# Token-major attention turned by DMA for three of eight batches, in a fused linear-attention and bilinear-FFN kernel

## Chip, cores, metric

One core of one Trainium2 chip. The metric is the device time of one execution in microseconds (us), median over several. All runs that are compared are fast unless a slow one is named (slow: over 1.5% above the fastest run of the same kernel). A *turn* below is a DMA transpose; an *eviction* takes a result out of a bank of PSUM; a DMA has *landed* when its semaphore says so; *head* and *tail* are the first microseconds of an execution and the part after the last matmul starts.

## The reference

```python
# q, k, v: (8 batches, 8 heads, 576 tokens, 64), fp32
kv  = einsum('bhsd,bhse->bhde', k, v)
out = einsum('bhsd,bhde->bhse', q, kv)
rms = sqrt(mean(out * out, axis=-1, keepdims=True) + 1e-06)
x   = (out / rms * g_norm) as (4608 tokens, 512)      # heads side by side
y   = ((x @ w_a) * (x @ w_b)) @ w_out                 # 512 -> 1536 -> 512
```

## The kernel before

The FFN is done in blocks of 512 tokens; blocks 1 to 8 use a seven-product scheme for 2 x 2 block matrices, with differences of x and of the weights made on VectorE. The attention of later batches is woven in between. TensorE (PE) needs x with the 512 features on the partitions, in ring buffers `xp`. So the attention is computed feature-major, two heads (128 features) and 288 tokens at a time:

```python
def x_mm(self, p, h, ps):            # out, transposed: features x 288 tokens
    nc.tensor.matmul(ps[:, 0:HF], lhsT=self.kvd[:, p, :], rhs=self.q[p][:, h*HF:(h+1)*HF], ...)
def sq_op(self, p, h, sq):           # ScalarE
    nc.scalar.activation(sq, self.x_ps[p, h][:, 0:HF], AF.Square)
def s_mm(self, p, h, ps):            # mean over 64 features: a product with a matrix of 1/64
    nc.tensor.matmul(ps[:, 0:HF], lhsT=ones, rhs=self.sq[p, h], start=True, stop=True)
def rs_op(self, p, h, rs):           # ScalarE
    nc.scalar.activation(rs, self.s_ps[p, h][:, 0:HF], AF.Abs_reciprocal_sqrt, bias=eps_t)
def xt_op(self, p, h):               # VectorE: x * g * rs, straight into xp
    nc.vector.scalar_tensor_tensor(out=xcols(...), in0=self.x_ps[p, h][:, 0:HF],
        scalar=g_col, in1=self.rs[p, h], op0=ALU.mult, op1=ALU.mult)
```

That is 8 times two matmuls of 288 columns for each batch. q comes through DRAM: cast by GpSimd's DMA, then turned by one DMA transpose on SyncE's queue (SP). The order on each engine is fixed ahead of time by a small list scheduler, `Plan`, which simulates the engines with durations given in the program; at run time only semaphores wait. PSUM is dealt out so:

```python
PB, PA, PO = Pool(banks[0:4]), Pool(banks[5:8]), Pool(banks[4:5])   # blocks, attention, output
...
issue_us, q_us, ld["kv_us"] = (15.4, 4.3, 13.0) if dep is None else (9.0, 5.0 if b == 3 else 1.8, 13.0)
ld["n"] = plan.add("POOL", issue_us, prio, issue, [(dep["qn"], 8.0)] if dep else [], [ld["k"], ld["v"]])
```

`kv_us` is the time after the load's issue at which the scheduler thinks k and v have landed.

Of the kernel before, what the change touches and what calls it, by code (L numbers as in the profile page):

```python
# [8 lines left out]
FP32 = mybir.dt.float32  # L9
# [6 lines left out]


class Pool:
    def __init__(self, tiles):
        self.tiles, self.holder = tiles, [None] * len(tiles)  # L20

    def pick(self, gone=()):
        best = (INF, 0)
        for i, b in enumerate(self.holder):
            if i not in gone:
                best = min(best, (b.freed() if b else 0.0, i))
        return best


# [11 lines left out]
class Buf:  # L41
# [6 lines left out]
    def take(self, t=0.0):  # L48
        r = self.ring
        i = r.pool.pick()[1]  # L50

        self.got = max(r.when(), r.pool.pick()[0])
        self.tile = r.pool.tiles[i]
        r.pool.holder[i] = self
        r.held = [b for b in r.held if b.freed() > t] + [self]
        return self

# [78 lines left out]
def kernel(  # L136
# [11 lines left out]
    nc = tc.nc  # L148
# [33 lines left out]
    EH = d_model // 2  # L182

    const = ctx.enter_context(tc.tile_pool(name="const", bufs=1))
    scr_pool = ctx.enter_context(tc.tile_pool(name="scr", bufs=B, space=bass.MemoryType.DRAM))
    psum = ctx.enter_context(tc.tile_pool(name="psum", bufs=1, space=bass.MemoryType.PSUM))
    ctx.enter_context(tc.manual_schedule())

    def sb(name, shape, dt):
        return const.tile(shape, dt, name=name)  # L190
# [15 lines left out]
    as_t = sb("as", [128, 4, NJ, 256], FP16)  # L206
    b_ts = [sb(f"c{i}", [128, 4, 2, NMAX], FP16) for i in range(2)]
    u_t = sb("u", [128, 6, 2, NMAX], FP32)
    sq_ts = [sb(f"sq{i}", [128, HF], BF16) for i in range(3)]
    rs_ts = [sb(f"rs{i}", [128, HF], FP32) for i in range(3)]  # L210
    o_ts = [sb(f"o_sb{i}", [128, 4, d_model], FP32) for i in range(2)]

# [203 lines left out]
        ]  # L416

    T0 = 20.0
    plan = Plan({"PE": 5.7, "DVE": 3.3, "ACT": 2.7, "SP": 5.0, "POOL": 22.5, "V": 0.0})
    PB, PA, PO = Pool(banks[0:4]), Pool(banks[5:8]), Pool(banks[4:5])  # L420
    RX, RY, RO = Ring(PB, 2), Ring(PB, 2), Ring(PO)
    RQ, RS = Ring(PA, 2), Ring(PA, 2)
    RU, RB, RAB = Ring([u_t[:, i] for i in range(6)]), Ring(b_ts), Ring(ab_ts)
    RT, RAS = Ring([T_t[:, i] for i in range(5)]), Ring([as_t[:, i] for i in range(4)])
    RSQ, RRS, ROS = Ring(sq_ts), Ring(rs_ts), Ring(o_ts)
    RK, RV, RQT, RKD = Ring(k_ts), Ring(v_ts), Ring(qT_ts), Ring(kvd)
    normed = {}
# [14 lines left out]
    def slices(at, win, extra):  # L442
        w0, w1 = win
        for i in range(2 * NP):
            p, h = divmod(i, 2)
            pr = w0 + (w1 - w0) * i / (2 * NP)
            x, s = ((Buf(RX), Buf(RY)) if at.b == 0 and i % 3 == 1 else (Buf(RQ), Buf(RS)))
            sq, rs = Buf(RSQ), Buf(RRS)
            ta = at.b * S + h * HF
            war = [  # L450
                n
                for j, (a, b) in enumerate(blocks_of)
                if a < ta - R + HF and b > ta - R
                for n in readers.get(j, ())
            ]
            n1 = plan.add(
                "PE", mm_us(1, HF), pr,
                lambda p=p, h=h, x=x: at.x_mm(p, h, x.tile), extra(p), [x], at.qt,
            )
            n2 = plan.add(  # L460
                "ACT", act_us(HF), pr, lambda p=p, h=h, b=sq: at.sq_op(p, h, b.tile), [n1], [sq]
            )
            n3 = plan.add(
                "PE", mm_us(1, HF), pr,
                lambda p=p, h=h, s=s: at.s_mm(p, h, s.tile), [n2], [s], [sq],
            )
            s_done[at.b] = n3
            n4 = plan.add(
                "ACT", act_us(HF, True), pr,
                lambda p=p, h=h, b=rs: at.rs_op(p, h, b.tile), [n3], [rs], [s],  # L470
            )
            normed[at.b, p, h] = plan.add(
                "DVE", dve_us(HF) + 0.06, pr,
                lambda p=p, h=h: at.xt_op(p, h), [n4] + war + ([g_n] if at.b == 0 else []), (), [x, rs],
            )

    def early_batch(b, win):
# [35 lines left out]
            done[p] = [n2, n4]  # L513
        slices(at, win, lambda p: done[p])

    def late_batch(b, load, win):
        at = Attn(b)
        w0, w1 = win
        kb, vb, qb = load["k"], load["v"], load["q"]
        kd = Buf(RKD)  # L520
        at.qt = [qb, kd]

        def view(t):
            return t[:, 0 : H * (NCH + 1) * D].rearrange("p (h c d) -> p h c d", h=H, d=D)

        s = Buf(RS)

        def kv_mm():
            kv_ps = s.tile[:].rearrange("p (a e) -> p a e", a=NP)
            for c in range(NCH + 1):  # L530
                for p in range(NP):
                    hs = slice(2 * p, 2 * p + 2)
                    nc.tensor.matmul(  # L533
                        kv_ps[:, p, :],
                        lhsT=kb.tile[:, c, hs, :],
                        rhs=view(vb.tile)[:, hs, c, :],
                        start=(c == 0 and p == 0),
                        stop=(c == NCH and p == NP - 1),
                    )

        n = plan.add(
            "PE", 1.15, w0, kv_mm, [(load["n"], load["kv_us"]), plan.at(w0 - 3)], [s, kd], [kb, vb]
        )

        def kv_out():
            kv_ps = s.tile[:].rearrange("p (a e) -> p a e", a=NP)
            at.kvd = kd.tile
            nc.scalar.copy(at.kvd[0:D, :, 0:D], kv_ps[0:D, :, 0:D])
            nc.scalar.copy(at.kvd[D:, :, D:], kv_ps[D:, :, D:])
            for p in range(NP):  # L550
                at.q[p] = qb.tile[:, p, :]

        m = plan.add("ACT", 0.75, w0, kv_out, [n], (), [s])
        slices(at, (w0 + 0.12 * (w1 - w0), w1), lambda p: [m, (load["qn"], 8.0)])


    def load_node(b, prio, dep):
        ld = {"k": Buf(RK), "v": Buf(RV), "q": Buf(RQT)}
        scr = scr_pool.tile([NP, S, 2, D], BF16, name="scr", tag="scr")

        def issue():
            if dep is not None:
                nc.gpsimd.tensor_copy(gate_t, dep["q"].tile[0:1, 0, 0:1])
            qv = q[b].rearrange("(p hl) s d -> hl s p d", hl=2)
            for hl in range(2):
                nc.gpsimd.dma_start(  # L566
                    out=scr[:, :, hl, :].rearrange("p s d -> s p d"), in_=qv[hl]
                )
            kt = ld["k"].tile
            ks = k[b, :, 0:SA, :].rearrange("h (sp c) d -> sp h c d", c=NCH)  # L570
            for c in range(NCH):
                nc.gpsimd.dma_start(out=kt[:, c], in_=ks[:, :, c, :])  # L572
            nc.gpsimd.dma_start(out=kt[0:SB, NCH], in_=k[b, :, SA:S, :].rearrange("h sp d -> sp h d"))
            for n, src in (("v", v),):
                t = ld[n].tile[:, 0 : H * (NCH + 1) * D].rearrange(
                    "p (h c d) -> p h c d", h=H, d=D
                )
                nc.gpsimd.dma_start(
                    out=t[:, :, 0:NCH, :],
                    in_=src[b, :, 0:SA, :].rearrange("h (sp c) d -> sp h c d", c=NCH),  # L580
                )
                nc.gpsimd.dma_start(
                    out=t[0:SB, :, NCH, :], in_=src[b, :, SA:S, :].rearrange("h sp d -> sp h d")
                )

        def transpose():
# [2 lines left out]
                in_=scr[:].rearrange("a s h d -> (a s) (h d)"),  # L589
            )  # L590

        issue_us, q_us, ld["kv_us"] = (15.4, 4.3, 13.0) if dep is None else (9.0, 5.0 if b == 3 else 1.8, 13.0)

        ld["n"] = plan.add(
            "POOL", issue_us, prio, issue, [(dep["qn"], 8.0)] if dep else [], [ld["k"], ld["v"]]
        )
        ld["qn"] = plan.add(
            "SP", 2.5, prio, transpose, [(ld["n"], q_us)], [ld["q"]]
# [95 lines left out]
    def wino_block(bi, win, wsum):  # L694
# [26 lines left out]
        for j in range(NJ):  # L721
# [4 lines left out]
            tkb = plan.add("V", 0.0, pr - 3, lambda: None, (), [bb])  # L726
            X = Buf(RQ if (bi == nb and j % 3 == 2) or (bi == 1 and j % 3 == 1) else RX)
            Y, Z = Buf(RY), Buf(RO if bi == 1 and j % 2 else RY)
            u1, u2, u3 = Buf(RU), Buf(RU), Buf(RU)
            wts = [(wa_t, sums["a"]), (wb_t, sums["b"])]  # L730

# [291 lines left out]
    for b in range(2, B):  # L1023
        t = b * S / N0
        at_win[b] = (max(53.0, st[int(t) - 1] + (t % 1) * L[int(t) - 1] - 18), st[int(t)] - 22 + (t % 1) * 12)
    loads = {2: load_node(2, 22.5, None)}
    wo_n = load_wo(loads[2])
    for b in range(3, B):
        loads[b] = load_node(b, at_win[b - 1][0], loads[b - 1])
    gb = Buf(RQ)  # L1030
    g_in = plan.add(
        "PE", 0.07, 8.5, lambda: nc.tensor.transpose(gb.tile[:, 0:1], g_row, one), [plan.at(6.4)], [gb]
# [10 lines left out]
    for bi in range(1, nb + 1):  # L1043
        o_win = (st[bi] + 1.0, st[bi + 1] - 1.0) if bi < nb else (st[bi] + O_A, st[bi + 1] + O_B)
        if bi == 1:
            o_std(ab, muls, (o_win[0] + 4.0, o_win[1] + 4.0))
            osum = out_sums(st[2] - 10)
        else:
            o_block(bi - 1, ab, muls, osum, o_win, 2, (RO, RY, RY), 1)
        for b in needs[bi]:  # L1050
            late_batch(b, loads[b], at_win[b])
        ab, muls = wino_block(bi, (st[bi], st[bi + 1]), wsum)
    o_block(
        nb, ab, muls, osum, (st[nb + 1], st[nb + 1] + o_us[nb]), NJ // 2,
# [38 lines left out]
```

## Time and profile before

| | before |
|---|---|
| median of the timed runs | 299.75 us (298.81 to 300.07, 4 runs) |
| span of the profiled run | 297.8 us |
| busy: PE, VectorE (DVE), ScalarE (ACT) | 98%, 79%, 65% |
| gaps between matmul starts, 40 to 130 us / 130 to 258 us | 1.50 / 0.25 us |
| from the start of the last matmul to the end | 4.96 us |

The gaps, here and below, are worked out from the trace: the distance from the start of one matmul to the start of the next, less its columns / 2.4 GHz, less 2.5 ns, summed where it is positive. They tell more than "busy", which models the ends of matmuls and fills such gaps. PE is fed almost without a break, so the count of columns sets the time.

### The profile page before, as it was taken

The numbers are of one execution on the slowest core, as the hardware profiler recorded it, in microseconds if no ns is written. First come the engines' busy times: TensorE is split into PE (matmuls) and PEld (weight loads), VectorE is DVE, ScalarE is ACT, GpSimd is POOL, SyncE is SP. The second block draws the span as 40 slices with busy tenths as digits, with TensorE's granted clock in tenths as the row PEclk, the third lists the DMA queues.
The fourth block names the chain that finished last, engine by engine and source line by source line (L and its number), as shares of the span: only waits on it lengthen the run. The fifth ranks groups of instructions, "written<-read, shape, count | busy, mean of one in ns | idle before, by whom it ended". The sixth has DMA issues, their size and how long they took to land.

```text
span 297.8 us, 6705 instructions
## 1 busy us (share of the span) xinstructions
PE 290.5 (98%) x2635; PEld 238.9 (80%) x2635; DVE 234.0 (79%) x435; ACT 192.4 (65%) x401; POOL 76.7 (26%) x95
## 2 busy tenths in 40 slices
PE   8999999999899999999999999999999999999993
PEld 3645559865788988889888988889888888888882
DVE  5544879894976998889779977997599859897762
ACT  3847767865588577866787658954996466654521
POOL 8945830940190650380560000000000000000000
PEclk9999999999999999999999999999999999999999
DMA  8999999799999699699999200020004001100043
GB/s 178 199 199 199 194 159 155 119 166 186 202 113 172 94 191 174 42 136 210 136 146 222 74 0 2 36 108 0 2 0 143 1 2 70 73 3 0 34 144 108
DMA packets 98195, 32.72 MB, mean 110 GB/s; under 512 B 74612, under 2 KB 94068, under 8 KB 98164
## 3 DMA queue, kind: packets, MB, share of 16 engines
q0 software_dynamic: 77552, 18.44, 65.3%
q1 hardware_dynamic: 20000, 13.16, 20.3%
q10 hardware_dynamic: 612, 0.71, 0.8%
q8 instruction: 20, 0.33, 0.5%
q14 instruction: 11, 0.09, 0.1%
HBM read 37.75 MB, written 12.98 MB: 170 GB/s over the span
## 4 chain that ended last, share of the span: by engine, by line
PE 71%; DMA 22%; POOL 4%; issue 1%; DVE 1%; ACT 0%; DVEq 0%; SPq 0%; POOLq 0%
PE bk L742 42%; PE bk L911 24%; DMA scr<-in_q_dram 8%; DMA v_t<-in_v_dram 4%; DMA wb_t<-in_moe_w_b_dram 4%; DMA qT<-scr 3%; DMA wa_t<-in_moe_w_a_dram 3%; PE bk L362 2%; PE bk L348 2%; PE bk L533 2%; POOL as L237 1%; POOL so L237 1%; POOL scr L566 1%; DVE o_sb L949 1%; POOL wo_t L609 1%
## 5 line engine op out<-in xcount | busy, mean ns | idle before, releaser
L761 DVE TENSOR_TENSOR c<-bk,u 128x512 f16<-128x512 f32 x144 | 96.6, 685 | 25.2 <-ACT u L415 12.8
L415 ACT COPY u<-bk 128x512 f32<-128x512 f32 x144 | 81.8, 590 | 37.3 <-PE bk L742 33.8
L742 PE MATMUL bk<-xp,wa_t 128*128 128x256 f16 x288 | 54.9, 273 | 0.0
L742 PE MATMUL bk<-xp,wb_t 128*128 128x256 f16 x288 | 54.9, 273 | 0.0
L371 DVE SCALAR_TENSOR_TENSOR xp<-bk,g_col,rs 128x288 f16<-128x288 f32 x64 | 32.4, 511 | 14.3 <-ACT rs L366 14.3
L742 PEld LDWEIGHTS <-wa_t 128*128 128x128 f16 x384 | 37.4, 98 | 5.7
L911 PEld LDWEIGHTS <-abt 128*128 128x128 f16 x384 | 37.4, 98 | 4.7 <-DVE abt L796 0.2
L742 PEld LDWEIGHTS <-wb_t 128*128 128x128 f16 x384 | 37.6, 98 | 4.4
L415 ACT CAST c<-bk 128x512 f16<-128x512 f32 x48 | 28.1, 590 | 17.7 <-PE bk L742 16.9
L911 PE MATMUL bk<-wo_t,abt 128*128 128x256 f16 x288 | 36.8, 273 | 0.0
L742 PE MATMUL bk<-T,sb 128*128 128x256 f16 x192 | 36.6, 273 | 0.0
L742 PE MATMUL bk<-T,sa 128*128 128x256 f16 x192 | 36.6, 273 | 0.0
L366 ACT ACTIVATE rs<-bk,eps_t 128x288 f32<-128x288 f32 x64 | 32.3, 508 | 5.7 <-PE bk L362 5.2
L796 DVE TENSOR_TENSOR abt<-c 128x1024 f16<-128x1024 f16 x48 | 32.9, 686 | 1.8
L742 PEld LDWEIGHTS <-sa 128*128 128x128 f16 x288 | 28.1, 98 | 3.8
L911 PEld LDWEIGHTS <-as 128*128 128x128 f16 x288 | 28.2, 98 | 3.5
L742 PEld LDWEIGHTS <-sb 128*128 128x128 f16 x288 | 28.2, 98 | 3.3
L943 ACT COPY o_sb<-bk 128x512 f32<-128x512 f32 x31 | 18.2, 587 | 15.2 <-PE bk L911 14.8
L358 ACT ACTIVATE sq<-bk 128x288 bf16<-128x288 f32 x64 | 25.5, 414 | 1.3 <-PE bk L348 0.6
L911 PE MATMUL bk<-so,as 128*128 128x256 f16 x192 | 25.5, 273 | 0.0
L572 POOL DMA_DIRECT2D k_t<-in_k_dram x24 | 21.2, 897 | 0.7 <-issue 0.5
L566 POOL DMA_DIRECT2D scr<-in_q_dram x12 | 19.6, 1637 | 2.6 <-issue 1.4
(99 smaller groups left out, 396.5 us busy)
## 6 DMA issues: line engine op xcount, KB each, us to landing
out_dram<-o_sb SPq DMA_DIRECT2D x20, 256.0 KB, 2.3
scr<-in_q_dram POOLq DMA_DIRECT2D x12, 288.0 KB, 8.2
k_t<-in_k_dram POOLq DMA_DIRECT2D x24, 128.0 KB, 8.8
v_t<-in_v_dram POOLq DMA_DIRECT2D x6, 512.0 KB, 10.9
out_dram<-o_sb SPq DMA_DIRECT2D x18, 128.0 KB, 2.4
wa_t<-in_moe_w_a_dram POOLq DMA_DIRECT2D x6, 256.0 KB, 10.7
wb_t<-in_moe_w_b_dram POOLq DMA_DIRECT2D x6, 256.0 KB, 10.9
wo_t<-in_moe_w_out_dram POOLq DMA_DIRECT2D x2, 768.0 KB, 9.4
```

Source lines behind the costliest of these rows:

```text
L237: nc.gpsimd.dma_start(out=t[n][:, hs, :, :], in_=src[b, hs].rearrange("h (sp c) d -> sp h c d", c=EC),)
L358: nc.scalar.activation(sq, self.x_ps[p, h][:, 0:HF], AF.Square)
L366: nc.scalar.activation(rs, self.s_ps[p, h][:, 0:HF], AF.Abs_reciprocal_sqrt, bias=eps_t)
L371: nc.vector.scalar_tensor_tensor(out=xcols(p, self.b * S + h * HF, HF), in0=self.x_ps[p, h][:, 0:HF], scalar=g_col, in1=self.rs[p, h], op0 ...
L415: ("ACT", act_us(n), lambda: nc.scalar.copy(*args())),
L566: nc.gpsimd.dma_start(out=scr[:, :, hl, :].rearrange("p s d -> s p d"), in_=qv[hl])
L572: nc.gpsimd.dma_start(out=kt[:, c], in_=ks[:, :, c, :])
L742: nc.tensor.matmul(ps.tile[:, i * n : (i + 1) * n], lhsT=lhs(w, sm)[:, kc, :], rhs=rhs()[:, kc, :], start=start and i == 0 and kc == 0, st ...
L761: lambda: nc.vector.tensor_add(cs(fi, h), full(ps), u.tile),
L796: nc.vector.tensor_mul(t, c[:, :, :, 0], c[:, :, :, 1])
L911: nc.tensor.matmul(ps.tile[:, sub * EH : (sub + 1) * EH], lhsT=lhs(slice(j, j + 1))[:, 0, sub * 128 : (sub + 1) * 128], rhs=rhs[:, j, :], ...
L943: lambda: nc.scalar.copy(o(fi, h), bank(X, every)), [dep], takes, frees,
```

## The change

Its intent: take matmul columns off PE. If a tile of the output is computed with tokens on the partitions, the sum of squares over a head's 64 features lies along the free axis, where VectorE can take it; the product with the matrix of ones goes away. The price is that x comes out the wrong way round. It is stored to DRAM, turned back by DMA transposes, and multiplied by g, which is per partition only after the turn, on ScalarE. This is done for batches 5 to 7 only. Blocks 5 to 7 get a fifth PSUM bank from the attention.

```diff
-    sq_ts = [sb(f"sq{i}", [128, HF], BF16) for i in range(3)]
+    sq_ts = [sb(f"sq{i}", [128, d_model], BF16) for i in range(2)]
+    ss_t = sb("ss", [128, 3, 2 * H], FP32)
+    xt_t = sb("xt", [128, 5, d_model], FP16)
...
+    B5, B6, CX, CY = 5, 8, 3, 4
+    TB, TURN, AHEAD = 5, 3.0, 8.0
+    PB5, PA5 = Pool(banks[0:4] + banks[7:8], PS), Pool(banks[5:7], PS)
...
+    def token_tiles(at, win, dep):
+        # for each of 5 tiles of 128 tokens (the last overlaps, 64 kept):
+        #   4 matmuls: X[:, p*128:(p+1)*128] = q[p][:, j0:j0+128].T @ kvd[:, p, :]
+        #   ScalarE: sq = Square(X)                       128 x 512
+        #   VectorE: ss = sum over each head's 64 columns 128 x 8
+        #   ScalarE: rs = Abs_reciprocal_sqrt(ss / 64 + eps)
+        #   VectorE: xt = X * rs
+        #   SP:      store xt to xs (DRAM)
+        def turn():
+            for p in range(NP):
+                nc.sync.dma_start_transpose(out=xcols(p, b * S, S), in_=xs[p])
+        n6 = plan.add("SP", 5.0, w1, turn, stored + war)
+        for i in range(4):
+            xg = xcols(i, b * S, S)
+            n7 = plan.add("ACT", act_us(S, True), w1, lambda xg=xg: nc.scalar.mul(xg, xg, g_col), [(n6, TURN)])
...
+            if xt is not None:      # load 7 only: wait for batch 5's turn
+                nc.gpsimd.tensor_copy(gate_t, xcols(NP - 1, (b - 2) * S, 1)[0:1])
...
-  ld["kv_us"] = (15.4, 4.3, 13.0) if dep is None else (9.0, 5.0 if b == 3 else 1.8, 13.0)
+  ld["kv_us"] = (15.4, 4.3, 13.0) if dep is None else (9.0, 5.0 if b == 3 else 1.8, 16.0 if b == 3 else 13.0)
...
+        if b >= TB:                 # plan this attention 8 us earlier
+            at_win[b] = tuple(x - AHEAD for x in at_win[b])
```

(The comment lines stand for the body of `token_tiles`.)

## The prediction

> **What bounds the kernel now.** I first read the page's busy table and its forty slices.
>
> ```profile
> PE 290.5 (98%) x2635; PEld 238.9 (80%) x2635; DVE 234.0 (79%) x435; ACT 192.4 (65%) x401; POOL 76.7 (26%) x95
> PE   8999999999899999999999999999999999999993
> ```
>
> PE is busy nearly everywhere; one slice near 74 us dips. As the ends of matmuls are modelled, I then looked in the timeline at how closely the starts follow one another where batch 5 is computed:
>
> ```profile
> 152.39 0.38 PE L742 MATMUL bk<-T,sa 128*128 128x256 f16 x2
> 152.61 0.38 PE L742 MATMUL bk<-T,sb 128*128 128x256 f16 x2
> 152.83 0.29 PE L362 MATMUL bk<-sq,ones 128*128 128x288 bf16 x1
> 152.95 0.29 PE L348 MATMUL bk<-qT,kvd 128*128 128x288 bf16 x1
> 153.07 0.60 PE L911 MATMUL bk<-wo_t,abt 128*128 128x256 f16 x4
> ```
>
> The starts are what counts: two matmuls of 256 columns every 0.22 us, one of 288 every 0.12 us. I added up all start-to-start distances against columns / 2.4 GHz. From 80 us to 290 us the excess is 0.23 to 0.29 us in every 10 us, some 2.5 ns for each matmul: TensorE is gapless there. So the kernel is bound by the number of columns it streams, and a bank of PSUM or an engine's free time is worth nothing unless PE waits for it. The one gap after the first 20 us is found in the timeline and in the table of waits:
>
> ```profile
> 76.90 1.06 PE L533 MATMUL bk<-v_t,k_t 128*128 128x128 bf16 x16
> 79.15 0.38 PE L533 MATMUL bk<-v_t,k_t 128*128 128x128 bf16 x4 [1.19 <-DMA v_t<-in_v_dram]
> 79.37 0.82 PE L911 MATMUL bk<-wo_t,abt 128*128 128x256 f16 x6
> ...
> PE bk L533 <- DMA v_t<-in_v_dram: 1.2, 1, 1.2
> ```
>
> That is the k-v product of batch 3, planned before the last piece of v has landed; start to start PE loses 1.36 us.
>
> The groups by shape give the cost of the parts that change:
>
> ```profile
> L371 DVE SCALAR_TENSOR_TENSOR xp<-bk,g_col,rs 128x288 f16<-128x288 f32 x64 | 32.4, 511 | 14.3 <-ACT rs L366 14.3
> L366 ACT ACTIVATE rs<-bk,eps_t 128x288 f32<-128x288 f32 x64 | 32.3, 508 | 5.7 <-PE bk L362 5.2
> L358 ACT ACTIVATE sq<-bk 128x288 bf16<-128x288 f32 x64 | 25.5, 414 | 1.3 <-PE bk L348 0.6
> L415 ACT COPY u<-bk 128x512 f32<-128x512 f32 x144 | 81.8, 590 | 37.3 <-PE bk L742 33.8
> L761 DVE TENSOR_TENSOR c<-bk,u 128x512 f16<-128x512 f32 x144 | 96.6, 685 | 25.2 <-ACT u L415 12.8
> ```
>
> and the question about the transposed tile gives the price of a turn by DMA of one batch:
>
> ```profile
> L587 SPq DMA_TRANSPOSE qT<-scr x6: 5503/6154/6463, 42.2 to 155.5; - x6
> DMA to landing us min/median/max: 7.5/9.9/11.9
> ```
>
> The queue is held for 6 us by the issue; the fastest landing, 7.5 us, is that of batch 7, when the loads have nearly ended.
>
> **What the Trainium skill says.** "TensorE: Matmul & The Clock Gate", section "Wait — 56ns, not 53.3ns?": warm matmuls start N / 2.4 GHz + about 2.5 ns apart. The trace agrees: 0.12 us for 288 columns, and in the chain of waits twenty of 128 columns (L533) take 1.12 us, 56 ns each. "ScalarE: Activation LUTs", section "What ACT_TABLE_LOAD costs": 186 ns + 0.833 ns per element, and some 93 ns for each per-partition operand. That gives 612 ns for 512 elements (trace: 590) and 520 ns for 288 with a bias column (trace: 508). "VectorE: DVE Perf Modes", section "The TRN2 errata — SBUF-src ops pay a fixed extra latency per instruction": (N + 151) / 0.96 ns for an fp32 tensor_tensor, so 691 ns at 512; the trace has 685. "DMA: Bandwidth & Descriptors", section "Anatomy of one DMA — SWDGE (gpsimd) path": a fixed part of some 2 us per DMA, mostly completion; the stores of this kernel, on the hardware queue, land after 2.3 us by the median.
>
> **The change part by part, for each of batches 5 to 7.**
>
> TensorE. Out go 8 products of 288 columns (L348) and 8 sums by the matrix of ones (L362): 16 x 0.1225 = 1.96 us. In come 5 token tiles x 4 matmuls of 128 columns: 20 x 0.056 = 1.12 us, the price of the 20 matmuls of L533, which also load new weights each time. Net -0.84 us, for three batches **-2.5 us**. All of it lies on the path, since PE is gapless.
>
> The stall of batch 3. The plan now puts its k-v product 3 us later (16 instead of 13 us after the load), so that other products fill the place: **-1.3 us**, if ready work is there; block 1's output products follow directly, so I think there is.
>
> ScalarE. Out: 8 x (414 + 508) = 7.4 us. In: 5 squares of 512 (0.59 each), 5 short reciprocal roots of 8 elements (280 + 7 = 0.29 by the skill's formula), 4 multiplications by g over 576 elements (280 + 480 = 0.76 by the same): 2.95 + 1.45 + 3.04 = 7.4 us. Nothing gained or lost; beside PE anyway.
>
> VectorE. Out: 8 x 0.511 = 4.1 us. In: 5 sums and 5 scalings over 512 elements, each taken as L761's 0.685: 6.9 us. Plus 2.8 us for each batch, in some 31 us of a block. In the windows 140 to 170, 170 to 201 and 201 to 232 us DVE is busy 84%; but the starts of back-to-back L761 are 0.60 us apart, not 0.685, so the real occupation is nearer 74%, and becomes some 82%. Beside PE, with room.
>
> DMA. In come 5 stores and 4 turns. After the last scaled row: 2.3 us for the store to land, 7.5 to 10 us for the turn, up to 3 us for the four multiplications by g. That is 13 to 15 us where L371 wrote x at once. The attention is planned 8 us earlier, so x is ready 5 to 7 us later than now in relation to the blocks. The plan books 2.2 + 8 us for store and turn, within the measured range. Batch 7's load waits for batch 5's turn; in the trace of before it is issued from 145 to 154 us and used from 205.6 us, so some 15 us of delay do no harm, and the turn has the DMA engines to itself.
>
> Banks. Blocks 5 to 7 get a fifth bank. PE waits for none now, so I book 0; it is there to absorb the jitter of a busier DVE.
>
> Sum: -2.5 - 1.3 = -3.8 us, from 299.7 to **295.9 us**. I add 0.4 us for new short waits and predict **296.3 us**, which is 1.1% less.
>
> **The rivals.**
>
> First: ScalarE stands waiting for the turn. Its order is fixed; if a turn lands later than the planned 8 us after issue, the multiplication by g holds up the evictions of PSUM behind it. Landings of 9.9 and 11.9 us in the trace speak for it; that those fell among heavy loads, and the gate on load 7, speak against. One overrun of 2 to 4 us, less the 1 to 2 us that free banks cover, costs 1 to 2 us; in all three batches 3 to 6 us: 299 to 302 us.
>
> Second: x comes too late for the block. Before, block 5's first difference starts at once when batch 5 is done:
>
> ```profile
> 158.13 0.51 DVE L371 SCALAR_TENSOR_TENSOR xp<-bk,g_col,rs 128x288 f16<-128x288 f32 x1
> 158.55 0.41 DVE L711 TENSOR_TENSOR T<-xp,xp 128x512 f16<-128x512 f16 x1
> ...
> 165.33 0.42 DVE L711 TENSOR_TENSOR T<-xp,T 128x512 f16<-128x512 f16 x1
> ```
>
> The differences are spread over 7 us, so they are not urgent at 158 us, and 5 us can be taken from that. Were they urgent, PE would wait up to 3 us in a block: 300 to 305 us. The first two products of a row don't need the differences, which speaks against.
>
> Third: VectorE becomes the bound in blocks 5 to 7. At 82% on average it should not be, but its work comes in bursts; waits of 0.5 us in a few places, 1 to 2 us in all: 297 to 298 us.
>
> Fourth, the other way: the new bank removes waits that the profile hides. The gapless starts leave nothing to remove; even all of the above can't give more than 4 us, so a gain above 2% (6 us) has no source.
>
> **Range and chances.** The low end, 294.8, is the whole gain, a quick run (before spread over 1 us) and a little from the shifted weave. The high end, 299.5, is the gain almost eaten by the first or third rival. Over 2% faster 0.03 (no source), over 2% slower 0.06 (the first two rivals together), the rest within 2%.
>
> **What would show it.** PE's instruction count should rise by 12 (60 in, 48 out), and the distances from start to start by no more than 2.5 ns each; the wait of L533 for v should be gone; the turns should land about 8 us after issue, and ScalarE's waits for them should be short. DVE's busy time should rise by some 8 us, ACT's stay. I am wrong if PE shows new gaps of over 2 us in all between 130 and 250 us, or if the stall near 77 us stays or moves elsewhere; the waits before ScalarE's multiplication and before the differences would tell which rival it was.

## The result

| | before | changed |
|---|---|---|
| median | 299.75 us (298.81 to 300.07, 4 runs) | 297.05 us (296.91 to 297.43, 4 runs) |
| ratio of fast runs | 1 | 0.9917 (95%: 0.9893 to 0.9941) |
| span of the profiled run | 297.8 | 294.8 |
| gaps of PE, 40 to 130 / 130 to 258 us | 1.50 / 0.25 | 0.42 / 0.51 |
| last matmul's start to the end | 4.96 | 5.27 |

A ratio is the mean time of one kernel's fast runs over that of the other's in the same rounds, so it is not quite the ratio of the medians quoted. The time fell by 2.7 us, 0.8 to 0.9%, inside the predicted range and 0.75 us above the predicted 296.3 us. The interval excludes 1.

The page of the changed kernel, busy table and slices of PE:

```profile
PE 288.1 (98%) x2646; PEld 238.1 (81%) x2648; DVE 240.2 (81%) x441; ACT 191.7 (65%) x395; POOL 77.1 (26%) x96
PE   8999999999999999999999999999999999999993
```

The dip near 74 us is gone. Two matmul records are missing here (2646 against 2648 weight loads); before, all 2635 were there. So the program has 13 matmuls more: 60 in, 48 out, and one of the dummies that keep PE busy at the start. DVE rose by 6 us, ACT stayed.

The timeline of PE around batch 3's k-v product in the changed kernel (start, us, what):

```profile
79.21 1.28 PE L624 MATMUL bk<-v_t,k_t 128*128 128x128 bf16 x20
80.33 0.38 PE L839 MATMUL bk<-T,wa_t 128*128 128x256 f16 x2
80.55 0.38 PE L839 MATMUL bk<-T,wb_t 128*128 128x256 f16 x2
81.03 1.14 PE L1008 MATMUL bk<-wo_t,abt 128*128 128x256 f16 x9
```

All twenty matmuls now run together, 2.3 us later than before. But between 80.55 and 81.03 two matmuls take 0.48 instead of 0.22 us: a small gap of 0.27 us has come in right after. It is there, with 0.26 to 0.27 us, in all twelve profiles of kernels that have the later k-v product. It ends 0.05 us after an eviction on VectorE (L858, 80.30 to 80.98 us), so PE probably waits for that bank; this was not tested.

The new groups, by shape (out, in, count, busy us, mean ns of one):

```profile
L539 PE MATMUL bk<-kvd,qT 128*128 128x128 bf16 x60 | 5.6, 219 | 0.0
L572 DVE TENSOR_TENSOR xt<-bk,ss 128x512 f16<-128x512 f32 x15 | 10.1, 681 | 0.0
L558 DVE TENSOR_REDUCE ss<-sq 128x8 f32<-128x512 bf16 x15 | 10.1, 676 | 0.3 <-ACT sq L554 0.3
L554 ACT ACTIVATE sq<-bk 128x512 bf16<-128x512 f32 x15 | 9.1, 606 | 0.4 <-DVE c L858 0.3
L600 ACT ACTIVATE xp<-xp,g_col 128x576 f16<-128x576 f16 x12 | 8.3, 766 | 0.0
L565 ACT ACTIVATE ss<-ss,eps_t 128x8 f32<-128x8 f32 x15 | 4.6, 308 | 2.1 <-DVE ss L558 2.0
```

L600 never waited: its idle time is 0.0. How that comes about is seen in ScalarE's timeline around the end of batch 5's turn:

```profile
159.24 0.59 ACT L1040 COPY o_sb<-bk 128x512 f32<-128x512 f32 x1
159.73 2.77 ACT L600 ACTIVATE xp<-xp,g_col 128x576 f16<-128x576 f16 x4
162.40 1.05 ACT L420 COPY u<-bk 128x512 f32<-128x512 f32 x2
```

and in the question about `xp`, its turns (issue time on the queue min/median/max in ns, then landing in us for one of four pieces):

```profile
L594 SPq DMA_TRANSPOSE xp<-xs x12: 1152/1254/2024, 153.4 to 219.4; - x12
DMA to landing us min/median/max: 2.6/2.7/4.1
```

Batch 5's four pieces were issued from 153.36 us; the last landed at 160.67 us, 7.3 us later. The four multiplications followed piece by piece and were over at 162.5 us.

**Where the time went.** In the span: fewer columns -2.5 us (48 x 122.5 ns less 60 x 56 ns); gaps from 40 to 130 us -1.1 us; new gaps from 130 to 258 us +0.3 us; the end +0.3 us. The sum is -3.0 us, the difference of the two spans. The 0.3 us at the end come after the last store has landed, which was 0.93 us before the end of the span and is now 1.23 us; in the last 1.5 us of the trace SP has 8 semaphore instructions where it had 4. In e1, without the new path, the same stretch takes 0.93 us; in all twelve profiles with the new path 1.16 to 1.64 us. So it comes with the new path; that the added DMAs and their semaphores are the reason is likely but was not tried alone.

### The profile page after: what moved, and what is told of

Same layout as the page of the kernel before. It is cut to its first block, busy times and chain, and to the rows that moved or that the text cites. A ratio compares the mean times of both kernels' runs of the same rounds, so it can differ in the third digit from the quotient of the medians.

```text
span 294.8 us, 6757 instructions
## 1 busy us (share of the span) xinstructions
PE 288.1 (98%) x2646; PEld 238.1 (81%) x2648; DVE 240.2 (81%) x441; ACT 191.7 (65%) x395; POOL 77.1 (26%) x96
## 4 chain that ended last, share of the span: by engine, by line
PE 93%; DVE 4%; issue 1%; ACT 1%; DVEq 0%; ACTq 0%
PE bk L839 47%; PE bk L1008 24%; PE bk L387 7%; PE bk L310 3%; PE bk L943 3%; PE bk L624 2%; PE bk L353 2%; PE bk L367 2%; PE bk L341 1%; PE bk L539 1%; PE bk L325 1%; DVE c L858 1%; DVE so L746 1%; DVE o_sb L1046 1%; DVE T L806 1%
## 5 line engine op out<-in xcount | busy, mean ns | idle before, releaser
L858 DVE TENSOR_TENSOR c<-bk,u 128x512 f16<-128x512 f32 x144 | 96.1, 684 | 19.3 <-PE bk L839 11.8
L420 ACT CAST c<-bk 128x512 f16<-128x512 f32 x48 | 28.0, 587 | 12.1 <-PE bk L839 11.5
L376 DVE SCALAR_TENSOR_TENSOR xp<-bk,g_col,rs 128x288 f16<-128x288 f32 x40 | 20.2, 512 | 10.9 <-ACT rs L371 10.9
L371 ACT ACTIVATE rs<-bk,eps_t 128x288 f32<-128x288 f32 x40 | 20.0, 506 | 6.2 <-PE bk L367 6.1
L1046 DVE TENSOR_TENSOR o_sb<-bk,o_sb 128x512 f32<-128x512 f32 (+1 forms) x25 | 16.4, 663 | 3.0 <-PE bk L1008 2.3
```

The lines of the kernel that those rows point to most:

```text
L376: nc.vector.scalar_tensor_tensor(out=xcols(p, self.b * S + h * HF, HF), in0=self.x_ps[p, h][:, 0:HF], scalar=g_col, in1=self.rs[p, h], op0 ...
L420: ("ACT", act_us(n), lambda: nc.scalar.copy(*args())),
L858: lambda: nc.vector.tensor_add(cs(fi, h), full(ps), u.tile),
L1046: nc.vector.tensor_add(o(fi, h, subs), bank(ps, subs), other)
```

## The experiments

All results were correct against the reference. PE's gaps are in us, as defined above. One run of e6 and one of e11 were slow; they are left out of the ratios, but are in the medians.

One thing makes the long waits of three of these runs dearer than they look. Near the end of a wait of PE of 3.9 us in e6, 4.1 us in e8 and 3.3 us in e11, a stretch of 3.4 us began in which PE's granted clock was 0.50 (e8 had a second such stretch soon after). Matmuls of 256 columns then started 0.21 instead of 0.11 us apart. By this count some 1.3 us of the gaps of e6, 2.4 us of e8 and 1.3 us of e11 are slow matmuls and not waits. After the longest wait in e4, 2.5 us, the clock stayed at 1.00.

| run | median us | ratio to before (95%) | span | gaps 40-130 | gaps 130-258 |
|---|---|---|---|---|---|
| e1_wait_only | 298.36 | 0.9960 (0.9947-0.9973) | 296.4 | 0.60 | 0.17 |
| e2_no_wait_fix | 297.33 | 0.9929 (0.9914-0.9943) | 295.2 | 0.54 | 0.60 |
| e3_four_banks | 297.22 | 0.9924 (0.9912-0.9936) | 295.5 | 0.42 | 1.84 |
| e4_ahead0 | 303.55 | 1.0145 (1.0126-1.0165) | 301.5 | 0.41 | 6.92 |
| e5_no_gate | 299.03 | 0.9985 (0.9973-0.9998) | 296.8 | 0.50 | 2.18 |
| e6_from4 | 304.35 | 1.0133 (1.0103-1.0164) | 302.8 | 1.12 | 8.24 |
| e7_g_dve | 297.68 | 0.9942 (0.9929-0.9955) | 296.1 | 0.42 | 1.19 |
| e8_from3 | 314.04 | 1.0479 (1.0449-1.0509) | 311.6 | 10.63 | 8.36 |
| e9_three_sq | 296.76 | 0.9904 (0.9890-0.9919) | 294.7 | 0.41 | 0.52 |
| e10_changed_again | 296.91 | 0.9909 (0.9892-0.9925) | 294.8 | 0.42 | 0.51 |
| e11_xt2 | 305.03 | 1.0150 (1.0096-1.0204) | 302.0 | 0.42 | 7.22 |
| e12_p4_last | 296.28 | 0.9887 (0.9873-0.9902) | 294.0 | 0.42 | 0.52 |

Runs e1, e2, e3, e6 shared one set of runs of the kernel before (median 299.47), e4, e5, e7, e8 a second (299.48), e9 to e12 a third (299.63).

### The two sources of the gain, one at a time

```diff
# e1: on the kernel before          (e2: the reverse, on the changed kernel); the end of the line
-    1.8, 13.0)
+    1.8, 16.0 if b == 3 else 13.0)
```

> The kernel before with one number changed: batch 3's k-v product is planned 16 us after its load instead of 13. My account (PE-column bound, one real stall of 1.36 us): the wait of PE for v near 77 us disappears, the span and the time fall by 1.2 to 1.4 us, to about 298.4 us (ratio 0.9955). Rival (the stall only moves: there is no ready work, or the later product delays block 3): within 0.3 us of before.

> The changed kernel with that one number set back to 13. My account: the token-major path alone is left, worth 60 x 56 ns in place of 48 x 122.5 ns, so 2.5 us: about 297.2 to 298.0 us when the changed kernel measures 297.0, with the wait of 1.2 us for v back near 77 us. Rival (the gain came mostly from the mended wait): 299 us or more, little better than before.

e1 came out at -1.1 us: the number alone mends the wait, as expected. In e2 the path alone gave -2.1 us, as expected too, but not all of the wait came back. Its timeline shows why (PE, changed kernel with the earlier plan):

```profile
77.28 1.28 PE L624 MATMUL bk<-v_t,k_t 128*128 128x128 bf16 x20
...
80.09 0.41 PE L353 MATMUL bk<-qT,kvd 128*128 128x288 bf16 x2 [0.23 <-DMA qT<-scr]
```

The product ran through at 77.28 us: v's last piece had landed at 77.45 us. A gap of 0.39 us came 2.3 us later instead, 0.23 us of it a wait for the turned q. In the profile of the kernel before it landed at 79.11 us. Over the fourteen profiles this landing falls between 76.8 and 79.7 us, with the same loads before it. So the wait is a matter of the single execution, between nothing and 1.4 us; planning the product at 79 us or later takes the luck out of it. The spread of the runs fits: 1.2 us over e2's six and 1.0 us over the eleven of the kernel before in the same rounds, against 0.24 us over e1's five and 0.5 us or less for the changed kernel. The two parts don't add up exactly: -1.1 and -2.1 us against -2.7 us together. On the changed kernel the later product brought only 0.3 to 0.4 us in the median (297.33 us against 296.91 and 297.05 us, from other rounds).

### What the fifth bank does

```diff
-    B5, B6, CX, CY = 5, 8, 3, 4
+    B5, B6, CX, CY = 99, 99, 3, 4
```

> The changed kernel with blocks 5 to 7 back on four PSUM banks; the attention keeps its two banks, so the eighth bank lies idle in these blocks. My account booked nothing for the bank, since PE waits for no bank: within 0.5 us of the changed kernel, 296.6 to 297.5 us. Rival (the busier VectorE needs the fifth bank to keep PE fed): new gaps on PE between 150 and 250 us of 1 us or more in all, 298 us or more.

The time stayed within half a microsecond, as expected from "nothing", yet the gaps are those of the rival: 1.84 us against 0.51 us from 130 to 258 us, eight gaps of 0.07 to 0.58 us where the changed kernel has two. Both are true because the schedule also ended in another order (a product of another kind last): from the last matmul's start to the end it took 4.21 us instead of 5.27 us, 1.06 us less, and that hid most of the loss (its head was 0.4 us later, too). With five banks the changed kernel has about 1.3 us less of gaps. Not all of that need be the bank itself, since the planner's order on PE, VectorE and ScalarE differs too: the gap of 0.34 us at 138.8 us lies in block 4, which has four banks in both kernels. The longest, 0.58 us at 227.6 us, is a wait for an eviction on VectorE, as a want of banks would show. That the bank seems worth only 0.2 us in time is an accident of the tail. The accident is used in the last experiment.

### How late x may come

```diff
-    TB, TURN, AHEAD = 5, 3.0, 8.0
+    TB, TURN, AHEAD = 5, 3.0, 0.0
```

> The changed kernel with the attention of batches 5 to 7 not planned 8 us earlier. In the changed kernel the differences of a block start at about the same time as before the change, so the 8 us just pay for the turn. If so, x is now some 8 us too late, part of which other work fills: PE gaps of 2 to 5 us at the start of each of blocks 5 to 7, 303 to 310 us. Rival (x has slack of 8 us and more before PE needs it, as the prediction's second rival was answered): within 1 us of the changed kernel.

6.6 us slower than the changed kernel (303.55 against 296.9 to 297.1): the 8 us are needed. (The edit moves the windows by which loads 6 and 7 are planned as well; load 7 began at 163.9 us instead of 161.3 us.) The timeline of block 6's start in this run, VectorE, ScalarE and PE:

```profile
196.69 2.77 ACT L600 ACTIVATE xp<-xp,g_col 128x576 f16<-128x576 f16 x4
199.50 0.42 DVE L806 TENSOR_TENSOR T<-xp,xp 128x512 f16<-128x512 f16 x1 [1.98 <-ACT xp L600]
199.99 0.38 PE L839 MATMUL bk<-T,wa_t 128*128 128x256 f16 x2 [2.55 <-ACT u L420]
```

The turn of batch 6 landed at 197.5 us here, the multiplications by g and then the eviction of a bank stood in line on ScalarE, and PE waited 2.55 us for that eviction. The first differences of blocks 5, 6 and 7 start at 162.9, 193.7 and 225.0 us in the changed kernel and 3.1, 5.8 and 10.7 us later here. Two points of the expectation were off: before the change they started at 158.6, 190.9 and 223.8 us, so not "at about the same time" but 4.4, 2.8 and 1.2 us earlier; and only one gap is of the expected size, the next being 1.1 and 0.9 us.

### What the gate on load 7 protects

```diff
-                loads[b] = load_node(b, at_win[b - 1][0], loads[b - 1], turned.get(b - 2))
+                loads[b] = load_node(b, at_win[b - 1][0], loads[b - 1])
```

> The changed kernel without the gate that holds load 7 back until batch 5's turn has landed; the orders of PE, VectorE and ScalarE are the same. Load 7 then runs from about 144 to 163 us, beside the stores and turns of batch 5. If the gate protects the turn: the last turn of batch 5 lands 2 to 5 us later than 160.7 us, ScalarE waits for it before its multiplication by g, and PE shows gaps of 1 to 3 us near 160 us: 298 to 300 us. Rival (the turn is paced by its issue on the queue, not by the DMA engines): landing within 1 us and time within 0.3 us of the changed kernel.

The orders of PE, VectorE and ScalarE are unchanged; on SP only the turn of load 7's q moves, to just after batch 5's turn. So this is a clean test. It cost 2 us. ScalarE's timeline around batch 5's turn, which answers to the three lines of the changed kernel above:

```profile
159.59 0.59 ACT L1040 COPY o_sb<-bk 128x512 f32<-128x512 f32 x1
161.48 1.69 ACT L600 ACTIVATE xp<-xp,g_col 128x576 f16<-128x576 f16 x2 [1.30 <-DMA xp<-xs]
163.43 1.51 ACT L600 ACTIVATE xp<-xp,g_col 128x576 f16<-128x576 f16 x2 [0.26 <-DMA xp<-xs]
164.84 1.05 ACT L420 COPY u<-bk 128x512 f32<-128x512 f32 x2
```

ScalarE stands waiting for the turn and then delivers its evictions 2.4 us later than with the gate (0.35 us of it a later start); PE shows one gap of 1.46 us at 163.9 us. This is the prediction's first rival, brought about on purpose. But it is not the turn that became slow: issue to last landing took 6.8 us (157.34 to 164.14 us) against 7.3 us. The turn was issued 4 us later, because the stores before it landed late among the loads: the fourth, issued at 148.4 us, landed at 153.66 us against 149.98 us with the gate. The expected lateness was right, its place in the chain was not. The gate does not remove the collision, either: it moves it. In the changed kernel load 7 is issued from 161.3 us and its last v lands at 181.0 us, among batch 6's stores, which take 3.1 to 7.1 us from issue to landing there and 2.0 to 2.2 us in e5. There it costs nothing, for a reason that e11 shows.

### More batches the new way

```diff
# e6 (e8: with 3 in both places)
-    B5, B6, CX, CY = 5, 8, 3, 4
-    TB, TURN, AHEAD = 5, 3.0, 8.0
+    B5, B6, CX, CY = 4, 8, 3, 4
+    TB, TURN, AHEAD = 4, 3.0, 8.0
```

> The changed kernel with token-major attention and five banks from batch 4 and block 4 on instead of 5. My account: another 0.84 us of PE columns saved, 296.2 us. Rival (the turns of batch 4 fall among the loads of batches 5 and 6, land late, and ScalarE waits for them): PE gaps of 1 to 4 us, 297 to 300 us.

> The changed kernel with token-major attention and five banks from batch 3 and block 3 on. My account of columns alone: 2 x 0.84 us less than the changed kernel, 295.4 us. Rival (loads, whose gates now hang on turns of batches 3 to 5, come late or the turns land late among them): PE gaps of several us, 298 us or more, most of them between 80 and 150 us.

Both lost: e6 by some 7 us, e8 by 17 us against the changed kernel. In e6 the cause of the longest gap, 4.1 us at 131.4 us, is seen on SP's queue, and on ScalarE:

```profile
108.17 1.19 SPq L579 DMA_DIRECT2D xs<-xt  x2
109.54 10.38 SPq L682 DMA_TRANSPOSE qT<-scr  x1
120.02 3.64 SPq L579 DMA_DIRECT2D xs<-xt  x3
126.92 5.64 SPq L594 DMA_TRANSPOSE xp<-xs  x4
```

```profile
131.31 2.22 ACT L600 ACTIVATE xp<-xp,g_col 128x576 f16<-128x576 f16 x3 [3.11 <-DMA xp<-xs]
```

Batch 4's attention falls into the loads of batch 5. The turn of batch 5's q held the queue for 10.4 us; three stores of x, whose rows were scaled at 112.2, 114.5 and 118.9 us, stood behind it until 120.0 us and later, and so did the turn. The columns saved (0.84 us for a batch) are small beside that. (Block 4's fifth bank and a gate on load 6 come with the edit; they were not tried apart.) In e8 batch 3's turn comes late in this way as well; block 3's products wait 4.1 us for its x, until 108.9 us, and everything that follows is planned on times that no longer hold: load 7 starts at 175.0 us, since its gate hangs on a late turn, and in each block ScalarE waits for turns while PE waits for the evictions behind it (2.7 us before 209.3 us, for one). Of three, four and five batches, each with the gate on its loads, only with three does no multiplication by g wait for its turn; one or two batches were not tried.

### Where g is multiplied

```diff
# the ends of both lines are cut
-    "ACT", act_us(S, True), w1, lambda xg=xg: nc.scalar.mul(xg, xg, g_col)
+    "DVE", 0.25, w1, lambda xg=xg: nc.vector.tensor_scalar_mul(xg, xg, g_col)
```

> The changed kernel with g multiplied on VectorE (12 instructions of 576 elements, fp16 in and out) instead of ScalarE. My account: both engines lie beside PE, so the time stays within 0.4 us of the changed kernel; ScalarE loses about 9 us of busy time, VectorE gains 3 to 5 us. Rival (ScalarE's or VectorE's place in the evictions matters): over 1 us either way, with PE gaps where the multiplications lie.

Between the two expectations: 297.68 us, some 0.7 us slower than the changed kernel (by the ratios 0.9942 against 0.9909 and 0.9917, from different rounds). The profiled run was the slowest of the four (298.23 us). ScalarE's busy time fell from 191.7 to 185.0 us, less than the 9 us expected, VectorE's rose from 240.2 to 242.8 us, and PE's gaps from 130 to 258 us from 0.51 to 1.19 us. VectorE does this multiplication faster (its starts are 0.28 us apart, ScalarE's 0.67), but it is the fuller engine (82% busy), and the longest new gap, 0.50 us at 224.7 us, is a wait for an eviction on VectorE. As the planner's orders changed too, the reason stays argued; in this comparison ScalarE is the better place, by a margin that rests on runs of different rounds.

### How many buffers the scaled rows need

```diff
-    xt_t = sb("xt", [128, 5, d_model], FP16)
+    xt_t = sb("xt", [128, 2, d_model], FP16)      # and range(2) in its ring
```

> The changed kernel with two instead of five buffers for the scaled rows; all engines and queues have the same order. In the changed kernel's trace stores of batch 6 waited on the queue behind the turn of q (a row scaled at 168.9 us landed at 176.8 us, one scaled at 172.4 us at 183.9 us), so with two buffers the scaling of the fourth tile would wait on VectorE for some 6 us, and PE soon after: gaps of 3 to 8 us in all, 300 to 305 us. Rival (the plan gave the same order, so two would do): within 0.5 us of the changed kernel.

305.03 us, one of the four runs slow. All orders are the same as in the changed kernel, so only the waiting differs. VectorE and PE near 184 us:

```profile
183.86 0.69 DVE L572 TENSOR_TENSOR xt<-bk,ss 128x512 f16<-128x512 f32 x1 [3.91 <-DMA xs<-xt]
184.47 0.68 DVE L1046 TENSOR_TENSOR o_sb<-bk,o_sb 128x512 f32<-128x512 f32 x1
...
185.20 0.58 PE L839 MATMUL bk<-xp,wa_t 128*128 128x256 f16 x2 [3.28 <-DVE o_sb L1046]
```

The scaling waits 3.9 us for a buffer whose store was held on the queue by the turn of q and landed at 183.7 us; PE waits 3.3 us behind it. A second gap of 1.8 us lies at 144.4 us. The scheduler, which books 2.5 us on SP for the turn of q that here held the queue for 7.8 us, gave the same order for two buffers. With five buffers, one for each tile of a batch, no scaling waits for a store (the idle time of L572 above is 0.0).

### The head, and an attempt at a better kernel

```diff
# e9: three buffers for the squares
-    sq_ts = [sb(f"sq{i}", [128, d_model], BF16) for i in range(2)]
+    sq_ts = [sb(f"sq{i}", [128, d_model], BF16) for i in range(3)]
# e12: that, and
-    p4 = prod(6 + 0.1 * i, W[i], a22, t4, True, [n4], [W[i]], subs=subs)
+    p4 = prod(6 + 0.1 * i, W[i], a22, t4, True, [n4, p3] if i else [n4], [W[i]], subs=subs)
```

> The changed kernel with three buffers for the squares again instead of two. In every profile with two buffers the first product with the sums of block 1's columns started at 45.6 to 46.3 us, in the two with three buffers at 45.2 and 45.6 us; ScalarE's squares of batch 0 come in pairs instead of threes there. My theory: the third buffer, which the change gave up, costs the first 20 us some 0.2 to 0.5 us; this kernel then is 0.2 to 0.5 us faster than the changed one in the same rounds. Rival (the scatter of the head is chance): no difference within 0.15 us, squares in threes but block 1 no earlier.

> The changed kernel itself once more, for comparison in the same rounds: 297.05 us within 0.3 us, ratio to the kernel before 0.990 to 0.993.

> An attempt at a better version: three buffers for the squares, and in the last block's output the second half of the fourth product made to come after the third. In the run with four banks the plan happened to end this way, and from the last matmul to the end took 4.2 instead of 5.2 us. If that tail is due to the order: 0.8 to 1 us faster than the run with three buffers alone, about 296 us. Rival (PE has nothing to fill the place with and waits): PE gaps in the last 10 us, no gain or a loss up to 1 us.

The repeat of the changed kernel gave 296.91 us, as expected. With three buffers batch 0's last reciprocal root ended at 16.86 us instead of 17.58 us (before the change: 16.64 us), ScalarE's squares came in threes again, but the first product with the sums of block 1's columns began at 45.59 us against 45.66 us, and the time fell by only 0.15 us, with ranges that just overlap (296.70 to 296.88 and 296.84 to 296.96). The lost buffer delays the head of ScalarE by 0.7 us, of which at most 0.15 us reached the end here, less than the theory asked. The theory is not quite dead: over the fourteen profiles the four kernels with three buffers began that product at 45.2 to 45.6 us, the ten with two at 45.6 to 46.3 us.

e12 is the best of all: 296.28 us (296.08 to 296.41), 0.6 us under the changed kernel in the same rounds, with ranges apart. The end of PE's timeline in the changed kernel, and in e12:

```profile
286.98 1.47 PE L1008 MATMUL bk<-so,as 128*128 128x256 f16 x12
...
288.29 1.47 PE L1008 MATMUL bk<-wo_t,as 128*128 128x256 f16 x12
```

```profile
286.23 1.47 PE L1008 MATMUL bk<-so,as 128*128 128x256 f16 x12
287.54 1.47 PE L1008 MATMUL bk<-wo_t,as 128*128 128x256 f16 x12
288.85 0.82 PE L1008 MATMUL bk<-so,abt 128*128 128x256 f16 x6
```

In the changed kernel all of PE's work is done before VectorE's last four additions are through, and VectorE ends at 291.06 us, 1.3 us after PE. In e12 six matmuls of another product come last, and VectorE adds up the rest beside them: it ends at 290.31 us, 0.6 us after PE. From the last matmul's start to the end of the span it is 4.60 us in place of 5.27 us. A gain of 0.5 us over e9 was measured where 0.8 to 1 was expected.

## Why the prediction was right

**What bounds the kernel.** Right. Every profile fits it: less PE's gaps after 40 us and the tail, the spans of the changed kernel and of its variants with three batches lie within 0.9 us of each other (288.3 to 289.1 us), those of the kernel before and e1 at 290.9 and 290.5 us.

**TensorE, -2.5 us.** Right. The 60 new matmuls start 56 ns apart (in the trace of the changed kernel, one group of L539 has starts at 165.40, 165.46, 165.51 and 165.57 us), and e2, where the path stands almost alone, measured -2.1 us by the medians, with the 0.3 us of the end and some 0.3 us of new gaps inside.

**The stall, -1.3 us.** Right in kind: e1 gives -1.1 us for the one number. It was a little over-sized: the wait is not the same in each execution (v's landing moves by up to 2.9 us between profiles; the prediction read one of them), and 0.27 us come back as a gap just after. The gaps from 40 to 130 us fell by 1.08, not 1.36 us.

**ScalarE, nothing.** Right: 5 x 606 + 5 x 308 + 4 x 766 ns = 7.6 us in a batch against the predicted 7.4, and its busy time moved by 0.7 us of 192.

**VectorE, +2.8 us a batch, with room.** Right by the mean durations: 5 x (676 + 681) ns = 6.8 us for 4.1 us. In the busy total it is 6.2 and not 8 us: the durations add up to 7.6 us more, and 1.4 us more of them overlap, which busy time counts once. No lasting bound came of it.

**DMA and the 8 us.** Right in kind, a little over-sized. From the end of the last scaling to the last product with g batches 5, 6 and 7 took 11.5, 11.3 and 11.6 us where 13 to 15 were predicted; the turns of batches 5 and 6 had landed 7.3 and 6.6 us after issue (the trace has no landing for the last piece of batch 7), where 7.5 to 10 were read from the turns of q beside the loads. The first difference of block 5 started at 162.9 us against 158.6 before, 4.4 us later, and PE still had work; e4 shows that 8 us more would not have been covered. The gate was right to be trusted, as e5 shows, though it protects the stores and not the turn.

**Banks, 0.** This step failed, if without harm to the sum. The reasoning "PE waits for none now" holds for the kernel before. In the changed kernel four banks give 1.84 us of gaps instead of 0.51 (e3); that the busier VectorE is the reason is likely, not shown. The prediction had named the use ("to absorb the jitter of a busier DVE") and not its size.

**What was missing** in the sum of -3.8 us, against -2.7 in the median and -3.0 in the spans: 0.3 us in the closing semaphores, 0.27 us next to the k-v product, 0.3 us of new gaps. The 0.4 us allowed for waits is met by the new gaps; the closing part was not thought of.

**The rivals.** The first was the real danger: it is what e5, e6 and e8 show when the loads are allowed near the stores and turns. It did not happen in the changed kernel: the multiplication by g never waited. The second is e4. The third showed only as gaps of 0.06 to 0.6 us, in e3 and e7. The fourth did not come: nothing was gained beyond the columns and the wait. That the total fell so near 296.3 us is in part luck: the 0.4 us allowed for waits came with no working, and v's landing decides what the stall is worth.

## What to carry to other kernels

Where TensorE's starts are gapless, only fewer columns make that stretch faster, and moving a reduction from a matmul by ones to another engine's free axis pays about those columns, if the layout can be turned back off the path. The turn's price here was latency in an in-order queue: plan it early, keep loads away from its stores, and give every tile in flight its own buffer. When a schedule is made by a planner, compare gaps and tail separately: any edit reshuffles the end, and a lucky order there can hide a loss elsewhere, or be kept on purpose.

## What the Trainium skill lacked or had wrong

- "DMA: Bandwidth & Descriptors", section "DMA Transpose (X-bar)", gives constraints but no time for which a transpose of these shapes holds the queue that issues it (elsewhere the page has only cycle counts of other shapes, in a comparison with a later chip). Here one of 2304 x 128 held SP's queue for 5.5 to 6.5 us in the kernel before, 10.4 us beside loads in e6, and 2.65 us in e5, where the loads had landed; one of 576 x 128 held it for 1.15 to 2.0 us (median 1.25). Stores behind it waited: one row of e6 was scaled at 112.2 us and its store not issued before 120.0 us.
- The same page, section "Anatomy of one DMA — SWDGE (gpsimd) path", has a fixed part of about 2 us, fitted to DMAs that GpSimd issues. The stores of scaled rows, issued by SP, took 2.0 us at best from issue to landing, but up to 7.1 us with loads in flight or a turn before them; the spread, not the fixed part, decided how many buffers were needed (e11).
- Nothing was wrong in the two formulas that the prediction used, that of "VectorE: DVE Perf Modes" and that of "ScalarE: Activation LUTs". They held for the new instructions: 681 ns for the scaling (691 by formula), 766 ns for g on 576 elements (760), 308 ns for 8 elements (287).
- No page that I found tells how the end of a program grows with what it issues ("Runtime: NRT & Kernel Launch" lists only the runtime's own closing steps). SP had 8 instead of 4 in the last 1.5 us, and the end came 0.3 us later after the last landing.
